# A second group of queries and keys by SyncE, and the first values one score visit earlier

## The chip, the cores and the metric

The kernel runs on one core of a Trainium2 chip. The core has a matrix engine (TensorE, PE in the profile), VectorE (DVE), ScalarE (ACT), GpSimd (POOL) and SyncE (SP), each with its own instruction stream; they wait for each other by semaphores. SP and POOL also issue DMAs. The metric is the device time of one execution in microseconds; the median of several runs is compared.

## The reference

Eight batches of sigmoid attention with 12 heads, 448 positions and head size 64, and behind it a two-layer block with a gate:

```
scores = q k^T / sqrt(64) - log(448)
attn   = 1 / (1 + exp(-scores))            # no sum over a row
x      = attn v, heads side by side        # 3584 x 768
h      = x w_in                            # 3584 x 2048
out    = (h / (1 + exp(-beta h))) w_out    # 3584 x 768
```

All inputs and the output are fp32. There is no softmax: each score is weighed by itself, so values can be taken as soon as a block of scores has passed ACT.

## The kernel before

All matrix products run in fp16 and add up in fp32. A *group* is four heads of one batch (three groups per batch, `QPB` = 3), which fill 128 partitions with 32 rows each when queries and keys are loaded as `[128, 14 x 64]`; a *slot* is two heads, so a group has two slots. `transpose` (line 173) turns 32x32 blocks on DVE and gives `qT` and `kT`; each transposed key tile takes two DVE instructions (lines 186 and 190).

`half_visit(g, c0, second)` (line 237) does half of a group's scores for half of the queries (224 columns): 16 matmuls into two score tiles, and then two ACT activations (`weigh`, line 209) that empty them into fp16. The pool of score tiles has three buffers in the first stage, so the third matmul of a visit waits until an activation two tiles back has ended. `attend(g, c0, n, part)` (line 255) multiplies with the values: 8 matmuls per slot, the last two of them with the last 64 rows of the values, and a DVE copy into `xTs`. `idle_units(n)` (line 518) puts n matmuls on zeros between the visits.

Until line 571 the order is written out by hand, engine by engine in program order (`tc.manual_schedule()`), and this is where the change is. Later stages go by a list of filler units (`dense1`, `dense2`, `strassen`) with costs, laid between the attention visits; none of that is edited.

Loads go two ways. SP's DMAs copy without a change of type: group 0's first half of queries and all of its keys come as fp32 into `staged`, a part of the later `gt` buffer, and are cast by DVE and ACT into `raws[0]` (lines 524 to 527). POOL's DMAs cast on the way (`load_one`, line 106; `load_v`, line 127): groups 1 and 2, then the six DMAs of the first batch's values (lines 131 and 138), then the second halves of the queries, then `w_in` in eight pieces. POOL's DMAs share eight semaphores in turn, so each waits before its issue for the landing of the one eight places ahead.

`double_v_last` (line 140) copies the last 64 rows of the values to the other 64 partitions, which odd slots need. Before, DVE does it after the transpose of group 0's second half of queries, and all values of the first half come after the last score visit of the pass.

Of the kernel before, what the change touches and what calls it, by code (L numbers as in the profile page):

```python
# [9 lines left out]
FP16 = mybir.dt.float16  # L10
# [3 lines left out]
def kernel(  # L14
# [10 lines left out]
    nc = tc.nc  # L25
# [3 lines left out]
    B, H, S, D = q.shape  # L29
    NTOK, DM = out.shape  # L30
    DFF = moe_w_in.shape[1]
    P = 128
    BLK = 32
    HQ = P // BLK
    NB = S // BLK
# [5 lines left out]
    QPB = H // HQ  # L41
# [5 lines left out]
    QH = S // 2  # L47
# [6 lines left out]
    rawp = ctx.enter_context(tc.tile_pool(name="rawp", bufs=3))  # L54
# [29 lines left out]
    def bank(name: str, cols: int = S, hold=None):  # L84
        i = min((i for i in used if i not in held.values()), key=used.get)
        touch(i)
        if hold is not None:
            held[hold] = i
        return psum["one"].tile([P, cols], FP32, tag=f"one{i}", name=name)
# [13 lines left out]
    raws = {}  # L103
    vs = {}

    def load_one(g: int, r: int, c0: int = 0, c1: int = NB):
        b, t = divmod(g, QPB)
        if g not in raws:
            raws[g] = rawp.tile([P, 2, NB, D], FP16, tag="raw", name="raw")
        nc.gpsimd.dma_start(  # L110
            out=raws[g][:, r, c0:c1].rearrange("p c d -> p (c d)"),
            in_=(q, k)[r][b, HQ * t : HQ * (t + 1)].rearrange("h (p c) d -> (h p) (c d)", c=NB)[
                :, c0 * D : c1 * D
            ],
        )
# [8 lines left out]
    def last_base(s: int) -> int:  # L124
        return (s % 2 ^ swapped(s // 2)) * KL

    def load_v(b: int):
        vs[b] = vp.tile([P, H, JF + 1, D], FP16, tag="v16", name="v16")
        rows = v[b].rearrange("h (p c) d -> p h (c d)", c=NB)
        for i in range(HQ):  # L130
            nc.gpsimd.dma_start(  # L131
                out=vs[b][i * BLK : (i + 1) * BLK, :, 0:JF].rearrange("p h j d -> p h (j d)"),
                in_=rows[:, :, JF * i * D : JF * (i + 1) * D],
            )
        rows = v[b].rearrange("h (p c) d -> p h c d", c=NB)
        for c in range(NF, NB):
            lo = (c - NF) * BLK
            nc.gpsimd.dma_start(out=vs[b][lo : lo + BLK, :, JF], in_=rows[:, :, c])

    def double_v_last(b: int):  # L140
        nc.vector.tensor_copy(out=vs[b][KL:P, :, JF], in_=vs[b][0:KL, :, JF])
# [27 lines left out]
    def in_order(b: int, t):  # L169
        t = t.rearrange("p c e -> p (c e)").bitcast(FP32)  # L170
        return t.rearrange("p (q c) -> p c q", c=NB) if b == B - 1 else t

    def transpose(g: int, r: int, c0: int = 0, c1: int = NB):
        raw = raws[g][:, r]
        if r == 0:
            if g not in qT:
                qT[g] = qTp.tile([P, NB * BLK, PAIR], FP16, tag="qT", name="qT")
            nc.vector.transpose(  # L178
                out=in_order(g // QPB, qT[g][:, c0 * BLK : c1 * BLK]),
                in_=raw[:, c0:c1].rearrange("p c d -> p (c d)").bitcast(FP32),  # L180
            )
            return
        kT[g] = kTp.tile([P, S, PAIR], FP16, tag="kT", name="kT")
        to = kT[g].rearrange("p k e -> p (k e)").bitcast(FP32)
        frm = raw.rearrange("p c d -> p (c d)").bitcast(FP32).rearrange("p (c f) -> p c f", c=NB)
        nc.vector.transpose(  # L186
            out=to[:, 0 : JF * P].rearrange("p (j i q) -> p i j q", j=JF, i=HQ),
            in_=frm[:, 0:NF].rearrange("p (i j) f -> p i j f", j=JF),
        )
        nc.vector.transpose(  # L190
            out=to[:, JF * P :], in_=frm[:, NF:].rearrange("p c f -> p (c f)")
        )
# [44 lines left out]
    def half_visit(g: int, c0: int, second: int):  # L237
        slots = (2 * g, 2 * g + 1)
        scos = [score_tile() for _ in slots]
        plan = [(s, jt, sco, jt * QH) for jt in (0, 1) for s, sco in zip(slots, scos)]  # L240
        widths = [S, S]
        if second:
            plan = [(s, 2, sco, 0) for s, sco in zip(slots, scos)]
            plan += [(s, JF, scos[0], QH) for s in slots]
            widths = [S, QH]
        for i in range(0, len(plan), 2):
            for e in range(PAIR):
                for s, jt, sco, u0 in plan[i : i + 2]:
                    for hh in range(2):
                        score(sco, u0, s, jt, hh, e, c0, QH)  # L250
        ats = {id(sco): weigh(sco, n) for sco, n in zip(scos, widths)}
        for s, jt, sco, u0 in plan:
            at_tiles[s, jt, c0] = ats[id(sco)][:, :, u0 : u0 + QH]

    def attend(g: int, c0: int, n: int, part=(0, 1)):
        b, t = divmod(g, QPB)
        if b not in xTs:
            xTs[b] = xTp.tile([P, NHC, S], FP16, tag="xT", name="xT")
        slots = [2 * g + x for x in part]
        avs = [bank("av_ps") for _ in slots]  # L260
        todo = [(s, av, jt) for s, av in zip(slots, avs) for jt in range(JF)]
        for s, av, jt in todo + [(s, av, JF) for s, av in zip(slots, avs)]:
            at = at_tiles.pop((s, jt, c0))
            base, nk = (last_base(s), KL) if jt == JF else (0, P)
            for hh in range(2):
                nc.tensor.matmul(  # L266
                    av[hh * D : (hh + 1) * D, 0:n],
                    vs[b][base : base + nk, 2 * (s % NPAIR) + hh, jt],
                    at[base : base + nk, hh, 0:n],
                    start=(jt == 0),  # L270
                    stop=(jt == JF),
                    tile_position=(base, hh * D),
                )
        for s, av in zip(slots, avs):
            nc.vector.tensor_copy(out=xTs[b][:, s % NPAIR, c0 : c0 + n], in_=av[:, 0:n])  # L275
# [215 lines left out]
    NH = NB // 2  # L491
    firsts = ctx.enter_context(ExitStack())
    share_psum(firsts, 3, 2)
    with tc.manual_schedule():
        raws[0] = rawp.tile([P, 2, NB, D], FP16, tag="raw", name="raw")
        wide = gt.rearrange("p a b -> p (a b)").bitcast(FP32)
        cut = NH * D
        early = [(0, 0, NH), (1, 0, NB)]
        staged = {}
        at = 0  # L500
        for r, c0, c1 in early:
            staged[r] = wide[:, at : at + (c1 - c0) * D]
            at += (c1 - c0) * D
            nc.sync.dma_start(  # L504
                out=staged[r],
                in_=(q, k)[r][0, 0:HQ].rearrange("h (p c) d -> (h p) (c d)", c=NB)[
                    :, c0 * D : c1 * D
                ],
            )
        nc.gpsimd.memset(dummy, 0.0)  # L510
        nc.scalar.activation(out=dummy, in_=dummy, func=AF.Sigmoid, bias=0.0, scale=1.0)
# [6 lines left out]
        def idle_units(n: int):  # L518
            for _ in range(n):
                nc.tensor.matmul(idle, still[:, 0:P], still, start=True, stop=True)  # L520

        idle_units(9)
        raw = raws[0].rearrange("p r c d -> p r (c d)")
        nc.vector.tensor_copy(out=raw[:, 0, 0:cut], in_=staged[0])
        transpose(0, 0, 0, NH)
        nc.scalar.copy(out=raw[:, 1, cut:], in_=staged[1][:, cut:])  # L526
        nc.vector.tensor_copy(out=raw[:, 1, 0:cut], in_=staged[1][:, 0:cut])
        transpose(0, 1)
        for g in range(1, QPB):
            load_one(g, 0, 0, NH)  # L530
            load_one(g, 1)
        load_v(0)
        nc.sync.dma_start(out=beta_in[0:NDC], in_=moe_beta.rearrange("(c p) -> c p", p=P))
        for g in range(QPB):
# [3 lines left out]
        for g in range(1, QPB):  # L538
            transpose(g, 0, 0, NH)
            transpose(g, 1)  # L540

        for g in range(QPB):
            for second in range(2):
                half_visit(g, 0, second)
                if 2 * g + second < 2 * QPB - 1:
                    idle_units(4 if g < QPB - 1 else 2)
        transpose(0, 0, NH, NB)
        double_v_last(0)
        attend(0, 0, QH, (0,))
        attend(0, 0, QH, (1,))  # L550
        half_visit(0, QH, 0)
        attend(1, 0, QH, (0,))
        attend(1, 0, QH, (1,))
# [120 lines left out]
```

## Time and profile before

| | |
|---|---|
| median of 3 runs | 387.36 us (387.35 to 389.22) |
| profiled execution | 387.25 us, span 385.5 us |
| PE busy | 379.1 us (98%) |
| DVE / ACT / POOL busy | 232.6 / 229.6 / 66.4 us |
| DMA, mean over the span | 90 GB/s |
| granted clock of PE | full in every slice |

The profile is of one execution. Its span is 1.75 us shorter than the time of the same execution, which also holds what lies before the first and after the last instruction. Busy times of the engines overlap, so only the chain that ended last, and the waits along it, say what a change can win.

Some events of the first 20 us, from the timelines and the DMA view (us from the start of the span):

| what | issued | landed | used by |
|---|---|---|---|
| group 0, queries / keys (SP) | 0.74 / 1.18 | 3.35 / 4.50 | scores at 5.75 |
| group 1, queries / keys (POOL) | 1.26 / 1.92 | 5.87 / 7.65 | scores at 8.93 |
| group 2, queries / keys (POOL) | 2.44 / 2.96 | 8.26 / 9.4 | scores at 12.14 |
| values, first / last of six (POOL) | 3.49 / 7.96 | 10.3 / 14.05 | values at 14.38 |
| group 0, second half of queries (POOL) | 8.56 | 14.27 | scores at 15.62 |
| `w_in`, first of eight (POOL) | 11.30 | 18.1 | first layer at 19.25 |

### The profile page before, as it was taken

To read this page: it belongs to the slowest core of one execution; us is meant where nothing else is said; L and a number is where in the kernel's file an instruction comes from. 1 tells how busy PE (TensorE), PEld (TensorE's weight loads), DVE (VectorE), ACT (ScalarE), POOL (GpSimd) and SP (SyncE) were. 2 spreads that over 40 slices of the span, in tenths; PEclk is the share of its full clock that TensorE was granted. 3 is DMA by queue.
4 is the path that set the end of the run, shared out by engine and by line. 5 is a ranking of instruction groups with operands and counts; after the bars stand their busy time and mean duration, and the time that the engine had idled before them with its cause. 6 is when DMAs were issued, how large, how long until landed. Compare 5 with 4: busy or idle time off the path is not lost.

```text
span 385.5 us, 7371 instructions
## 1 busy us (share of the span) xinstructions
PE 379.1 (98%) x2987; PEld 190.8 (49%) x2987; DVE 232.6 (60%) x439; ACT 229.6 (60%) x330; POOL 66.4 (17%) x114
## 2 busy tenths in 40 slices
PE   7999999999999999999999999999999999999996
PEld 3477744444554444444554445544455444555553
DVE  4356365875765657555764667755675665655762
ACT  5897855697364785487364783477762777535200
POOL 7832443140110410140110410113100000000000
PEclk9999999999999999999999999999999999999999
DMA  8999999737363930564363660639303300030033
GB/s 165 177 196 204 198 205 202 168 48 73 49 129 76 124 54 2 129 81 40 49 129 83 88 76 8 130 84 118 49 0 83 83 3 2 0 83 0 0 83 122
DMA packets 42401, 34.64 MB, mean 90 GB/s; under 512 B 21872, under 2 KB 38656, under 8 KB 42368
## 3 DMA queue, kind: packets, MB, share of 16 engines
q0 software_dynamic: 36688, 22.47, 42.9%
q1 hardware_dynamic: 5680, 11.71, 11.6%
q8 instruction: 23, 0.38, 0.4%
q14 instruction: 10, 0.08, 0.1%
HBM read 45.62 MB, written 11.01 MB: 147 GB/s over the span
## 4 chain that ended last, share of the span: by engine, by line
PE 95%; ACT 2%; DMA 1%; issue 0%; DVE 0%; SPq 0%; ACTq 0%
PE m_ps L284 38%; PE m_ps L396 29%; PE sco L200 12%; PE av_ps L266 10%; PE m_ps L314 5%; ACT attnT L211 2%; PE idle_ps L520 1%; DMA gt<-in_k_dram 1%; DVE kT L186 0%; ACT raw L526 0%; ACT sg L292 0%; DVE osb L327 0%; DVE gt L295 0%; SPq L504 0%; ACTq L292 0%
## 5 line engine op out<-in xcount | busy, mean ns | idle before, releaser
L211 ACT ACTIVATE attnT<-sco 128x896 f16<-128x896 f32 (+1 forms) x171 | 145.2, 902 | 85.2 <-PE sco L200 84.5
L284 PE MATMUL m_ps<-xT,w_in 128*128 128x448 f16 (+1 forms) x864 | 154.7, 332 | 0.2 <-DVE gt L295 0.2
L295 DVE TENSOR_TENSOR gt<-m_ps,sg 128x448 f16<-128x448 f32 (+1 forms) x144 | 81.8, 573 | 81.1 <-ACT sg L292 77.2
L284 PEld LDWEIGHTS <-w_in 128*128 128x128 f16 x864 | 80.6, 98 | 70.7 <-issue 15.3
L292 ACT ACTIVATE sg<-m_ps,beta_sb 128x448 f32<-128x448 f32 (+1 forms) x144 | 84.5, 597 | 36.2 <-PE m_ps L284 30.9
L396 PEld LDWEIGHTS <-sum 128*128 128x128 f16 x480 | 45.2, 98 | 36.2 <-issue 7.9
L200 PE MATMUL sco<-qT,kT 32*128 32x448 f16 (+3 forms) x864 | 52.1, 340 | 1.4 <-DVE kT L186 1.0
L396 PE MATMUL m_ps<-w_T,sum 128*128 128x384 f16 x288 | 51.6, 327 | 0.0
L110 POOL DMA_DIRECT2D raw<-in_q_dram x26 | 14.3, 550 | 186.2 <-DVE kT L190 179.9
L415 DVE TENSOR_TENSOR osb<-m_ps,osb 128x384 f32<-128x384 f32 x60 | 33.3, 556 | 18.7 <-PE m_ps L396 16.8
L266 PE MATMUL av_ps<-attnT,v 128*64 128x448 f16 (+3 forms) x432 | 42.1, 340 | 0.0
L275 DVE CAST xT<-av_ps 128x448 f16<-128x448 f32 (+1 forms) x54 | 28.8, 568 | 17.8 <-PE av_ps L266 17.7
L385 DVE TENSOR_TENSOR sum<-gt 128x1024 f16<-128x1024 f16 x60 | 39.2, 678 | 0.1
L396 PE MATMUL m_ps<-w_T,gt 128*128 128x384 f16 x192 | 34.2, 326 | 0.0
L396 PE MATMUL m_ps<-w_out,sum 128*128 128x384 f16 x192 | 33.7, 326 | 0.0
L266 PEld LDWEIGHTS <-v 128*64 128x64 f16 (+1 forms) x432 | 19.0, 107 | 24.6 <-issue 17.1
L200 PEld LDWEIGHTS <-kT 32*128 32x128 f16 (+1 forms) x864 | 13.4, 96 | 29.4 <-issue 27.1
L396 PEld LDWEIGHTS <-gt 128*128 128x128 f16 x192 | 18.1, 98 | 14.8 <-issue 3.1
L314 PE MATMUL m_ps<-w_out,gt 128*128 128x384 f16 (+2 forms) x128 | 22.5, 327 | 0.0
L131 POOL DMA_DIRECT2D v<-in_v_dram x32 | 19.8, 631 | 9.8 <-DMA w_in<-in_moe_w_in_dram 5.3
L178 DVE STREAM_TRANSPOSE qT<-raw 128x448 f32<-128x448 f32 (+1 forms) x27 | 16.6, 617 | 4.2 <-DMA raw<-in_q_dram 4.1
L314 PEld LDWEIGHTS <-gt 128*128 128x128 f16 x128 | 11.9, 98 | 10.3 <-issue 3.1
(26 smaller groups left out, 95.3 us busy)
## 6 DMA issues: line engine op xcount, KB each, us to landing
out_dram<-osb SPq DMA_DIRECT2D x98, 96.0 KB, 1.9
raw<-in_k_dram POOLq DMA_DIRECT2D x23, 224.0 KB, 4.5
raw<-in_q_dram POOLq DMA_DIRECT2D x21, 224.0 KB, 3.8
v<-in_v_dram POOLq DMA_DIRECT2D x32, 144.0 KB, 6.2
w_in<-in_moe_w_in_dram POOLq DMA_DIRECT2D x8, 384.0 KB, 10.7
w_out<-in_moe_w_out_dram POOLq DMA_DIRECT2D x4, 768.0 KB, 13.7
v<-in_v_dram POOLq DMA_DIRECT2D x16, 48.0 KB, 6.4
out_dram<-osb SPq DMA_DIRECT2D x2, 384.0 KB, 2.3
```

What stands on the lines that cost most here:

```text
L131: nc.gpsimd.dma_start(out=vs[b][i * BLK : (i + 1) * BLK, :, 0:JF].rearrange("p h j d -> p h (j d)"), in_=rows[:, :, JF * i * D : JF * (i + ...
L200: nc.tensor.matmul(sco[base : base + nk, hh, u0 : u0 + n], kT[g][lo : lo + BLK, jt * P : jt * P + nk, e], qT[g][lo : lo + BLK, c0 : c0 + n ...
L211: nc.scalar.activation(out=at[:, :, 0:n], in_=sco[:, :, 0:n], func=AF.Sigmoid, bias=NEG_LOG_S, scale=MSCALE,)
L266: nc.tensor.matmul(av[hh * D : (hh + 1) * D, 0:n], vs[b][base : base + nk, 2 * (s % NPAIR) + hh, jt], at[base : base + nk, hh, 0:n], start ...
L275: nc.vector.tensor_copy(out=xTs[b][:, s % NPAIR, c0 : c0 + n], in_=av[:, 0:n])
L284: nc.tensor.matmul(m1[:, 0:n], w_in16[:, hc, dc * P : (dc + 1) * P], xTs[b][:, hc, c0 : c0 + n], start=(hc == 0), stop=(hc == NHC - 1),)
L292: nc.scalar.activation(out=sg[:, 0:n], in_=m1[:, 0:n], func=AF.Sigmoid, bias=0.0, scale=beta_sb[:, dc : dc + 1])
L295: nc.vector.tensor_tensor(out=gt[:, dc, off : off + n], in0=m1[:, 0:n], in1=sg[:, 0:n], op=ALU.mult)
L314: nc.tensor.matmul(m2, gt[:, dc, cols(t)], w_out16[:, dc, lo:hi], start=(dc == 0), stop=(dc == NDC - 1),)
L385: nc.vector.tensor_tensor(out=sums[t, i], in0=x, in1=y, op=op)
L396: nc.tensor.matmul(m2, (x if op is None else sums[t, i])[:, dc], w[:, dc], start=first and dc == 0, stop=(dc == ND - 1), skip_group_check= ...
L415: nc.vector.tensor_tensor(out=out, in0=in0, in1=in1, op=op)
```

## The change

Group 1's first half of queries and its keys are no longer cast on the way by POOL's DMAs. SP loads them as fp32 behind group 0's, into the next part of the `gt` buffer, and DVE casts them into `raws[1]` (448 and 896 elements per partition) ahead of its transposes of that group. POOL's queue begins with group 2. In the last group of the first pass, the two idle matmuls between its visits are left out; the values of group 0's first slot take that place, ahead of the last score visit, and those of its second slot follow that visit. DVE doubles the last value rows ahead of the transpose of group 0's second half of queries.

```diff
-        raws[0] = rawp.tile([P, 2, NB, D], FP16, tag="raw", name="raw")
+        for g in range(2):
+            raws[g] = rawp.tile([P, 2, NB, D], FP16, tag="raw", name="raw")
...
-        early = [(0, 0, NH), (1, 0, NB)]
+        early = [(g, r, (NH, NB)[r] * D) for g in range(2) for r in range(2)]
...
-        for r, c0, c1 in early:
-            staged[r] = wide[:, at : at + (c1 - c0) * D]
-            at += (c1 - c0) * D
+        for g, r, n in early:
+            staged[g, r] = wide[:, at : at + n]
+            at += n
             nc.sync.dma_start(
-                out=staged[r],
-                in_=(q, k)[r][0, 0:HQ].rearrange("h (p c) d -> (h p) (c d)", c=NB)[
-                    :, c0 * D : c1 * D
-                ],
+                out=staged[g, r],
+                in_=(q, k)[r][0, g * HQ : (g + 1) * HQ].rearrange(
+                    "h (p c) d -> (h p) (c d)", c=NB
+                )[:, 0:n],
             )
...
         transpose(0, 1)
-        for g in range(1, QPB):
-            load_one(g, 0, 0, NH)
-            load_one(g, 1)
+        raw = raws[1].rearrange("p r c d -> p r (c d)")
+        nc.vector.tensor_copy(out=raw[:, 0, 0:cut], in_=staged[1, 0])
+        nc.vector.tensor_copy(out=raw[:, 1], in_=staged[1, 1])
+        load_one(2, 0, 0, NH)
+        load_one(2, 1)
         load_v(0)
...
+        double_v_last(0)
+        transpose(0, 0, NH, NB)
         for g in range(QPB):
             for second in range(2):
                 half_visit(g, 0, second)
-                if 2 * g + second < 2 * QPB - 1:
-                    idle_units(4 if g < QPB - 1 else 2)
-        transpose(0, 0, NH, NB)
-        double_v_last(0)
-        attend(0, 0, QH, (0,))
-        attend(0, 0, QH, (1,))
+                if g < QPB - 1:
+                    idle_units(4)
+                else:
+                    attend(0, 0, QH, (second,))
         half_visit(0, QH, 0)
```

More of the change, by code (lines that the diff above doesn't have):

```diff
@@ L523 @@
         raw = raws[0].rearrange("p r c d -> p r (c d)")
-        nc.vector.tensor_copy(out=raw[:, 0, 0:cut], in_=staged[0])
+        nc.vector.tensor_copy(out=raw[:, 0, 0:cut], in_=staged[0, 0])
         transpose(0, 0, 0, NH)
-        nc.scalar.copy(out=raw[:, 1, cut:], in_=staged[1][:, cut:])
-        nc.vector.tensor_copy(out=raw[:, 1, 0:cut], in_=staged[1][:, 0:cut])
+        nc.scalar.copy(out=raw[:, 1, cut:], in_=staged[0, 1][:, cut:])
+        nc.vector.tensor_copy(out=raw[:, 1, 0:cut], in_=staged[0, 1][:, 0:cut])
         transpose(0, 1)
-        for g in range(1, QPB):
-            load_one(g, 0, 0, NH)
-            load_one(g, 1)
+        raw = raws[1].rearrange("p r c d -> p r (c d)")
[3 more added lines that the diff above has]
+        load_one(2, 1)
         load_v(0)
```

## The prediction

> **What bounds the kernel now.** I read the page first (busy time and the chain that ended last), then busy time by stage, then the chain of the first 50 us in order of time, and last the timelines of ACT, DVE and POOL around the lines that move.
>
> ```profile
> span 385.5 us, 7371 instructions
> ...
> PE 379.1 (98%) x2987; PEld 190.8 (49%) x2987; DVE 232.6 (60%) x439; ACT 229.6 (60%) x330; POOL 66.4 (17%) x114
> ...
> PE 95%; ACT 2%; DMA 1%; issue 0%; DVE 0%; SPq 0%; ACTq 0%
> ```
>
> TensorE (PE) is busy nearly throughout and holds 95% of the chain. By stage (PE is the second number and the first busy time):
>
> ```profile
> 0.00:16.00 16.00, 13.65 (x155) 5.64 (x155) 5.92 (x17) 11.26 (x15) 12.36 (x24) 1.00 1.14 173
> 16.00:45.00 29.00, 28.96 (x366) 21.07 (x356) 16.07 (x47) 22.77 (x42) 11.08 (x18) 1.00 1.41 194
> ...
> 90.00:370.00 280.00, 280.00 (x2041) 135.72 (x2039) 175.14 (x313) 164.88 (x231) 28.66 (x50) 1.00 0.37 62
> ```
>
> From 16 us on PE stops for almost nothing, so what the change does before 16 us is carried to the end one for one, and nothing later can be won. The chain there (start, length, what):
>
> ```profile
> 1.18 3.31 DMA gt<-in_k_dram
> ...
> 8.03 0.97 PE idle_ps L520 x4
> 8.99 0.63 PE sco L200 x16
> ...
> 12.79 0.93 ACT attnT L211
> 13.71 0.04 issue
> 13.75 0.69 PE sco L200 x14
> 14.45 1.24 PE av_ps L266 x16
> 15.69 0.51 PE sco L200 x14
> 16.20 1.86 PE av_ps L266 x24
> ```
>
> The reader is to see that scores wait for ScalarE (ACT) to empty a score tile (12.79 to 13.71), and only then come the first values (14.45). ACT itself runs without a real pause here: its 12 activations of the first pass fill 9.49 us from 6.36. The last lines are of the timelines of ACT, DVE and POOL (start, length, in brackets the wait before):
>
> ```profile
> 14.50 1.35 ACT L211 ACTIVATE attnT<-sco 128x896 f16<-128x896 f32 x2
> 7.69 0.58 DVE L186 STREAM_TRANSPOSE kT<-raw 128x384 f32<-128x384 f32 x1 [1.42 <-DMA raw<-in_k_dram]
> 14.28 0.41 DVE L178 STREAM_TRANSPOSE qT<-raw 128x224 f32<-128x224 f32 x1 [4.14 <-DMA raw<-in_q_dram]
> 3.49 2.50 POOL L131 DMA_DIRECT2D v<-in_v_dram  x4
> 7.96 0.61 POOL L138 DMA_DIRECT2D v<-in_v_dram  x1 [1.21 <-DMA raw<-in_k_dram]
> ```
>
> **PE: two idle matmuls less, eight value matmuls earlier.** Before, from the end of the score visit at 12.76: two idle matmuls 0.54, two score matmuls and the wait for ACT until 13.75 (0.45), the rest of the visit 0.63 (14.38), 16 value matmuls 1.24 (15.62), the next score visit 0.51 (16.13). After: 8 value matmuls 0.62 (13.38); the same wait until 13.75, since the ninth activation, begun at 12.79, still frees its tile then; 0.63 to 14.38; 8 value matmuls 0.62 (15.00). Now the next visit comes too early. Its third matmul needs the tile of the eleventh activation, which begins at 14.50; the ninth took 0.96 from its start to the release of PE, so 15.46; the 14 matmuls left at 0.51/16 each take 0.45: 15.91. The gain is 16.13 - 15.91 = 0.22 us, out of the 0.54 + 0.18 (the wait proper) = 0.72 that stood there. The rest turns into a new wait for ACT at about 15.1.
>
> **SP and DVE: does group 1 come in time?** SP issues two more DMAs (0.38 and 0.42 us in the rows of group 0) at about 1.6 and 2.1; beta's moves from 1.65 to about 2.5, landed in 3.8, and is first used at 19.67, so it costs nothing. The queue moved 672 KB of group 0 from 1.75 to about 3.9, at 360 to 460 GB/s once it ran; at 400 the next 672 KB take 1.7, ending at 5.6, and landing follows by 0.6 as for group 0's keys (4.50 against 3.9): 6.2. That is the lower bound. The upper: if POOL's queue takes half from 3.9 on, 672 KB at 200 GB/s take 3.4, landing 7.9. After landing DVE casts 128x896: not in the trace; 128x448 took 0.395, of which 0.18 is fixed (transposes of 224 and 448 elements took 0.41 and 0.63), so 0.61, at most 2 x 0.395 = 0.79. Then transposes: 0.41, and 0.63 from kT's start to PE (5.12 to 5.75 for group 0). In all 1.71 (1.89). PE wants group 1 at 8.93, so landing by 7.22 (7.04) costs nothing and 7.9 costs 0.7 to 0.85. I take the low value: POOL's first data appear at 3.7, 2.4 us after its first issue at 1.26, where on idle queues they came 1.2 after (154.56, data at 155.8). So POOL's queue moved nothing while SP's streamed. The query cast (0.395) sits before this and is covered by the wait for the keys. Queued behind the casts on DVE are only group 2's transposes, wanted at 12.14 and ready at 10.13 before: 2 us of cover.
>
> **POOL: are the values there at 12.8?** POOL loses two issues (0.67 + 0.54), so the six value DMAs start at 2.44, not 3.49, and all go out by about 6.0, as the ring of eight no longer makes the last wait for group 1's keys (1.21 in the row above). The DMA view has the last value load issued at 7.96 and landed 6.1 later, 14.05. Ahead of it stood 1344 KB on this queue, now 1008; 336 KB at the 180 GB/s of 8 to 12 us are 1.9 less, and the start comes 1.7 later behind SP's stream: 13.85. But POOL's queue ran slowly from 3.65 to 7.0 (0.44 MB, 131 GB/s) while POOL was writing; with the writing done before it starts, 0.44 MB at 180 saves 0.9: 12.95. I take the middle, 13.4, since the row of 154.56 shows both, about 120 GB/s at first and 190 to 215 within a microsecond. The need: the last two matmuls of the early values (at 13.23) wait for v's last rows; after them 0.15, a score visit of 0.69 and 0.05 of latency must be over at 14.5, so landing by 13.6 costs nothing. Each microsecond later costs one, and the gain is gone at 13.82. Queries of the second half are issued once group 2's queries land, about as before, landed at 14.27 and are wanted at 15.0: cover 0.3 after 0.35 of copy and 0.41 of transpose. Weights of the first layer landed at 18.1 and are used at 19.25; their queue position in time is unchanged.
>
> **Sum.** -0.22. The profiled execution (387.25, span 385.5) would be 387.03; the median of the runs, 387.36, stands 0.11 above it, so 387.1. A measurement of this kernel tells some 0.5% (1.9 us) from no change, far more than this.
>
> [...] When casts ran at 3.35 and 4.52, the value issues beside them took 0.616 to 0.670, and 0.61 without. [...] SP's stream left POOL's queue waiting 1.2 us. [...]
>
> **The rivals.**
> 1. The values are late and PE, in order, holds the last score visit behind them. For: before, they landed only at 14.05. Against: 336 KB less ahead. At 13.95 it gives +0.1, at 14.6 +0.8 (388.2); slower than before from 13.82 on.
> 2. Group 1 is late. Under a fair share it lands at 7.9: 0.7 to 0.85 late, less 0.22: +0.5 to +0.6 (387.9). For: eight DMAs are queued beside it. Against: the 3.7.
> [...]
> 4. ACT's release is not the bound and the whole 0.72 is won: 386.6. Against: the 13.71 line.
> That the change does not do what it says is excluded by the order of the instructions: loads, casts and value matmuls stand where the text puts them.
>
> **Chances.** Forecast (within 0.25 of 387.1) 0.47; rival 1 0.25, of it 0.05 beyond 389.3; rival 2 0.13, 0.01 beyond; rival 3 0.08, 0.04 beyond; rival 4 0.02; 0.05 for a gain over 0.5% that no row shows. So faster 0.05, same 0.85, slower 0.10. The range runs from rival 4's 386.6 to 388.6, which takes in rival 2 and most of rival 1; the forecast's own is 386.9 to 387.4.
>
> **What would show it.** Right: score visits of group 1 still at 8.9, a wait for ACT of about 0.3 at 15.1, values of the second group at 15.9. [...]

## The result, and the profile after

The changed kernel takes 390.72 us (median of 6, 389.45 to 392.01) against 387.36 us before, a ratio of 1.0077 with a 95% interval of 1.0056 to 1.0098: slower, by 2.2 to 3.8 us, where 0.22 us less was forecast, too little to tell from no change. The profiled execution is the lowest of the six, 389.45 us with a span of 387.7 us, so the profile shows 2.2 us of the loss, and the other executions lose more. First the page of the kernel after, with the same lines as shown of before:

```profile
span 387.7 us, 7370 instructions
...
PE 381.1 (98%) x2985; PEld 190.9 (49%) x2985; DVE 233.1 (60%) x441; ACT 229.4 (59%) x330; POOL 65.4 (17%) x112
...
PE 93%; ACT 2%; DMA 2%; DVE 1%; issue 0%; SPq 0%; ACTq 0%
```

The span grew by 2.2 us, and the chain now holds 2% of DMA and 1% of DVE where it held 1% and none. Busy time by stage (start and end of the stretch, its length, busy time and instructions of PE, PE's weight loads, DVE, ACT and POOL, then the granted clock, the DMA share and GB/s) says where:

```profile
0.00:16.00 16.00, 13.58 (x115) 4.89 (x116) 5.92 (x17) 8.90 (x12) 11.18 (x22) 1.00 1.11 191
16.00:45.00 29.00, 28.67 (x376) 20.87 (x374) 15.84 (x45) 24.31 (x45) 10.62 (x17) 1.00 1.39 193
90.00:370.00 280.00, 280.00 (x2049) 135.08 (x2046) 174.56 (x313) 165.62 (x232) 28.77 (x50) 1.00 0.38 63
```

From 90 to 370 us PE is as full as before. In the first 16 us it issued 115 matmuls where it had issued 155, in nearly the same busy time, since some of them were slow (below). The chain of the first 50 us of the kernel after:

```profile
2.12 7.87 DMA gt<-in_k_dram
9.99 0.02 issue
10.01 0.63 DVE raw L532
10.64 0.32 DVE qT L178
10.96 0.47 DVE kT L186
11.43 0.05 issue
11.47 0.58 PE sco L200 x15
...
15.30 2.64 ACT attnT L211 x3
17.94 0.04 issue
17.98 0.57 PE sco L200 x11
18.55 1.87 PE av_ps L266 x24
```

The line to look at is the first. Group 1's keys, issued by SP at 2.12, land at 9.99; through POOL they had landed at 7.65. Behind them stand the cast and the transposes, and group 1's scores begin at 11.47, 2.54 later than the 8.93 of before. The values of the second group, which began at 16.13, begin at 18.48: 2.35 later. From there on the two kernels run in step, and the spans differ by 2.2.

In this execution not all of the 2.54 is the keys'. PE's first matmuls were slow: the four idle matmuls at 6.86 took 1.89 us, where they take 1.04 in the kernel before. Before (start, length, in brackets the wait):

```profile
6.26 1.04 PE L520 MATMUL idle_ps<-still 128*128 128x512 f16 x4
...
8.93 0.69 PE L200 MATMUL sco<-qT,kT 32*128 32x224 f16 x16
```

After:

```profile
6.86 1.89 PE L521 MATMUL idle_ps<-still 128*128 128x512 f16 x4
...
9.69 1.34 PE L521 MATMUL idle_ps<-still 128*128 128x512 f16 x4
11.47 0.58 PE L200 MATMUL sco<-qT,kT 32*128 32x224 f16 x16 [0.44 <-DVE kT L186]
```

PE was through with its own work only at 11.03 and waited 0.44 us for the keys. A second profile of the changed kernel, of an execution of 390.69 us and so close to the median, shows the keys' part by itself. There PE ran at its usual pace, was through at 9.72, and waited 2.97 us for keys that DVE could begin to cast only at 11.23 (DVE, then PE):

```profile
11.23 0.63 DVE L532 CAST raw<-gt 128x896 f16<-128x896 f32 x1 [2.59 <-DMA gt<-in_k_dram]
...
8.69 1.04 PE L521 MATMUL idle_ps<-still 128*128 128x512 f16 x4
12.69 0.58 PE L200 MATMUL sco<-qT,kT 32*128 32x224 f16 x16 [2.97 <-DVE kT L186]
```

### The profile page after: what moved, and what is told of

Same layout as the page of the kernel before. It is cut to its first block, busy times and chain, and to the rows that moved or that the text cites. A ratio compares the mean times of both kernels' runs of the same rounds, so it can differ in the third digit from the quotient of the medians.

```text
span 387.7 us, 7370 instructions
## 1 busy us (share of the span) xinstructions
PE 381.1 (98%) x2985; PEld 190.9 (49%) x2985; DVE 233.1 (60%) x441; ACT 229.4 (59%) x330; POOL 65.4 (17%) x112
## 4 chain that ended last, share of the span: by engine, by line
PE 93%; ACT 2%; DMA 2%; DVE 1%; issue 0%; SPq 0%; ACTq 0%
PE m_ps L284 38%; PE m_ps L396 29%; PE sco L200 11%; PE av_ps L266 10%; PE m_ps L314 5%; ACT attnT L211 2%; DMA gt<-in_k_dram 2%; PE idle_ps L521 1%; SPq L505 0%; DVE raw L532 0%; DVE kT L186 0%; ACT sg L292 0%; DVE osb L327 0%; DVE gt L295 0%; DVE qT L178 0%
## 5 line engine op out<-in xcount | busy, mean ns | idle before, releaser
L200 PE MATMUL sco<-qT,kT 32*128 32x448 f16 (+3 forms) x864 | 53.0, 344 | 1.8 <-DVE kT L186 1.2
L178 DVE STREAM_TRANSPOSE qT<-raw 128x448 f32<-128x448 f32 (+1 forms) x27 | 16.5, 615 | 0.1
```

Source lines behind the costliest of these rows:

```text
L200: nc.tensor.matmul(sco[base : base + nk, hh, u0 : u0 + n], kT[g][lo : lo + BLK, jt * P : jt * P + nk, e], qT[g][lo : lo + BLK, c0 : c0 + n ...
```

## The experiments

The theory formed from the two traces (A): SP's and POOL's loads share the DMA engines, so group 1's keys come late, and their lateness is the loss. The rivals: the new order costs PE the time (B); SP's queue is slow for its second pair of loads by itself (C). A further theory, on the spread between executions, is called D below.

**Each half of the change alone.** First the order without the loads:

```diff
+        double_v_last(0)
+        transpose(0, 0, NH, NB)
         for g in range(QPB):
             for second in range(2):
                 half_visit(g, 0, second)
-                if 2 * g + second < 2 * QPB - 1:
-                    idle_units(4 if g < QPB - 1 else 2)
-        transpose(0, 0, NH, NB)
-        double_v_last(0)
-        attend(0, 0, QH, (0,))
-        attend(0, 0, QH, (1,))
+                if g < QPB - 1:
+                    idle_units(4)
+                else:
+                    attend(0, 0, QH, (second,))
```

> The loads of the kernel before, with only the order of the change: no idle matmuls in the last group, the first slot's values ahead of the last score visit, the last value rows doubled before the transpose. Theory A (the whole loss is group 1's keys landing late, because SP's and POOL's queues share the DMA engines): scores of group 1 start at 8.9 us as before; the last value rows land at about 14.05, so the early values hold the last visit for 0.2 to 0.5 us; 387.3 to 387.9 us in all. Theory B (the new order costs PE the time, by values that block the visit behind them): 389 us or more.

Measured: 387.68 us (10 executions) against 387.70, ratio 1.0001 (0.9985 to 1.0017). The order alone costs and wins nothing that can be measured. B falls.

Then the loads and casts of the change with the order of before (the same lines the other way round):

> The loads and casts of the change with the order of the kernel before. Theory A: group 1's keys land at about 10.0 us, its scores start at about 11.5, and the time is that of the changed kernel plus the 0.2 us of the order, 389.6 to 392 us. Theory B: 387.2 to 387.6 us.

Measured: 392.74 us (4 executions, 389.83 to 393.88) against 387.70, ratio 1.011 (1.0065 to 1.0155). The whole loss comes with the loads, and more than expected. DVE could begin the cast of the keys only at 10.99 in its profile, and group 1's scores began at 12.45. This profile also shows something that the profile of the changed kernel hides, a fall of the granted clock. By stretch, the clock being the number ahead of the last two:

```profile
8.00:9.00 1.00, 1.00 (x12) 0.31 (x4) 0.37 (x1) 1.00 (x2) 0.00 (x0) 1.00 1.23 246
9.00:10.00 1.00, 0.21 (x1) 0.00 (x0) 0.03 (x1) 0.65 (x2) 0.00 (x0) 1.00 1.54 193
10.00:11.00 1.00, 0.00 (x0) 0.00 (x0) 0.01 (x1) 0.00 (x0) 0.55 (x1) 1.00 1.61 188
11.00:12.00 1.00, 0.00 (x0) 0.00 (x0) 1.00 (x3) 0.00 (x0) 0.24 (x1) 0.53 1.82 175
12.00:13.00 1.00, 0.55 (x16) 0.44 (x16) 1.00 (x4) 0.00 (x0) 1.00 (x2) 0.50 1.63 187
...
16.00:17.00 1.00, 1.00 (x11) 0.31 (x4) 0.00 (x0) 0.73 (x1) 1.00 (x2) 0.50 1.31 157
17.00:18.00 1.00, 1.00 (x7) 0.17 (x9) 0.00 (x0) 0.62 (x2) 1.00 (x3) 0.56 1.32 165
18.00:19.00 1.00, 1.00 (x19) 0.39 (x19) 0.00 (x0) 0.43 (x1) 0.85 (x2) 1.00 1.29 146
```

PE stood idle from 9.2 to 12.45, waiting for the keys. About two microseconds into the pause the clock fell to half and stayed there until about 17.9, for 6.8 us: the price of the pause goes on after it ends.

**The queues apart.** POOL's queue is held back until group 1's keys are in:

```diff
+        nc.gpsimd.tensor_copy(out=dummy, in_=staged[1, 1][:, 0:1])
         load_one(2, 0, 0, NH)
```

> The changed kernel, but POOL reads one element of group 1's staged keys before its first DMA, so its queue is empty while SP's four loads run. Theory A: alone on the engines, group 1's keys land at 6.2 to 6.6 us and its scores start at 8.9 to 9.0; the values start some 5 us later and their last rows land at 15.5 to 16.5, which now costs 2 to 3 us, so the time stays at 389 to 390.5. Rival C (SP's queue is slow for its second pair of loads by itself, whatever POOL does): keys still land at 9 or later.

Measured, in one execution: DVE begins the cast of the keys at 6.78 instead of 10.01, and group 1's scores begin at 8.96. C falls, and A's first half holds: the same four loads on the same queue, alone, bring the keys 3.2 us earlier. The timelines of DVE and PE (start, length, in brackets the wait before):

```profile
6.78 0.63 DVE L532 CAST raw<-gt 128x896 f16<-128x896 f32 x1 [0.65 <-DMA gt<-in_k_dram]
...
8.96 0.69 PE L200 MATMUL sco<-qT,kT 32*128 32x224 f16 x16
...
16.83 0.48 PE L266 MATMUL av_ps<-attnT,v 128*64 128x224 f16 x6 [3.77 <-DMA v<-in_v_dram]
```

The time is 394.84, some 4 us more than expected: PE waited 3.77 for the values, whose last rows came at 17.7 instead of 15.5 to 16.5, and the granted clock averaged 0.987 over the execution: at 18.03 a score visit of 16 matmuls took 1.07 us, at 12.48 it had taken 0.58.

**Less on SP.** Group 1's keys go back to POOL's queue, in its first place, and only the queries (224 KB) stay on SP:

```diff
-        early = [(g, r, (NH, NB)[r] * D) for g in range(2) for r in range(2)]
+        early = [(0, 0, NH * D), (0, 1, NB * D), (1, 0, NH * D)]
...
-        nc.vector.tensor_copy(out=raw[:, 1], in_=staged[1, 1])
+        load_one(1, 1)
         load_one(2, 0, 0, NH)
```

> The changed kernel with group 1's keys back on POOL's queue, in its first place, and only group 1's queries (224 KB) on SP. Theory A: sharing the engines with 224 instead of 672 KB, the queries land at 6 to 7 us, the keys at 6.5 to 7.6, group 1's scores start at 8.9 to 9.1, the last value rows land at 13.4 to 14; 387.0 to 387.5 us. Theory B: 389 us or more. Rival C: queries at 8 or later, scores at 9.5 or later, 388 us.

Measured: 388.28 us (10 executions, 387.38 to 389.37) against 387.70, ratio 1.0008 (0.9992 to 1.0024). The time is above what A gave, and the times of landing were missed by more: DVE could cast the queries only at 9.34, where 6 to 7 was expected. A load of a third of the size, alone on its queue from 3.9 on, still took until 9.3. The scores began at 10.80 in the profile, where PE, slow at first in this execution too, came to them without a wait. These numbers are the ones that C had given (8 or later, 9.5 or later, 388). But C has the queue slow whatever POOL does, and in the run before SP's second pair came early as soon as POOL's queue was empty. What is wrong in A is the size: the share that SP gets beside POOL is smaller than equal parts of 400 GB/s. From 5 to 8 us SP's packets took 27.9% of the engines' time here, POOL's 71.8%.

**POOL a little later.** POOL's queue waits for group 0's queries only:

```diff
+        nc.gpsimd.tensor_copy(out=dummy, in_=staged[0, 0][:, 0:1])
         load_one(2, 0, 0, NH)
```

> The changed kernel, but POOL reads one element of group 0's staged queries (landed at 3.35 to 3.5) before its first DMA, so its queue starts at about 4.0 and its first data come at 5.2 or later, when SP's loads are nearly over. Theory A (the queues take turns on the engines): group 1's keys land at 6.3 to 7.0 us and its scores start at 8.9 to 9.1; the last value rows land at 13.5 to 15, so 387.1 to 388.5 us in all, 2 to 3 us below the changed kernel. If it isn't the turns: keys at 9 or later and 389 us or more.

Measured: 388.19 us (12 executions) against 387.50 for before and 390.69 for the changed kernel on the same chip; ratio to before 1.0033 (1.0004 to 1.0061). The cast of the keys begins at 6.88 in the profile, as A expects. Group 1's scores begin at 9.30, 0.2 later than A gave, but PE came to them only then and did not wait for the keys. What is left is the values, which now land at 14.38 and hold the last score visit, as the first rival of the prediction had it:

```profile
13.14 0.48 PE L266 MATMUL av_ps<-attnT,v 128*64 128x224 f16 x6
14.43 0.28 PE L266 MATMUL av_ps<-attnT,v 64*64 64x224 f16 x2 [0.81 <-DMA v<-in_v_dram]
14.64 0.70 PE L200 MATMUL sco<-qT,kT 32*128 32x224 f16 x16
```

Three of the twelve stand at 390.77 to 392.33 with a granted clock of 0.987 to 0.991; the other nine have a median of 388.0.

The same loads with the order of before, where the values come after the last score visit:

> POOL's queue started after group 0's queries, as in the run before, but with the order of the kernel before (values after the last score visit, two idle matmuls). Theory A: keys at 6.8 to 6.9 us; the last value rows land at 14.0 to 14.6, and the values start at 14.4 to 15 without holding a score visit: 387.2 to 387.8 us for most executions, 0.3 to 0.6 below the same loads with the new order, and fewer executions with a granted clock below 0.995. If the late values are not the rest of the loss: 388.2 us as with the new order.

Measured: 387.69 us (11 executions, 387.13 to 387.98) against 387.60, ratio 0.9998 (0.9986 to 1.0009), and no granted clock below 0.998. With the queues apart and no early values, the loss is gone altogether. This also says that group 1's loads on SP and its casts on DVE cost nothing by themselves that can be measured.

**Lateness without the loads.** The kernel before, with eight unneeded transposes on DVE ahead of group 1's:

```diff
+        junk = const.tile([P, 448], FP32, name="junk")
+        for _ in range(8):
+            nc.vector.transpose(out=junk, in_=raws[0][:, 1].rearrange("p c d -> p (c d)").bitcast(FP32))
         for g in range(1, QPB):
             transpose(g, 0, 0, NH)
```

> The kernel before with eight unneeded transposes of 128x448 on DVE (some 4.6 us) ahead of group 1's, so that group 1's scores start at 11.0 to 11.7 us as in the changed kernel, with the loads of the kernel before. Theory A with D: 389.4 to 392 us, with the same spread and clocks as the changed kernel, since only the lateness counts. If the loss lies elsewhere in the change: below 388.5 us.

Measured: 392.13 us (6 executions, 390.32 to 392.76), ratio 1.0100 (1.0072 to 1.0127). The transposes took 5.36 us together, more than meant, and the scores began at 12.04 in the profile. The loads were those of before, so the lateness alone makes a loss of this size, whoever causes it. The median lies a little above the 392 that A with D gave. Five of the six had a granted clock of 0.990 to 0.996, and the one at 1.000 was the lowest.

The changed kernel again, on the same chip as the last one and the first run below:

> The changed kernel again, on the same chip as the others: 389.4 to 392 us.

Measured: 390.69 us (7 executions, 389.57 to 391.64). The four with a granted clock of 1.000 lie between 389.57 and 390.69, the three at 0.995 to 0.996 between 390.89 and 391.64. At a full clock the landing of the keys makes a spread as well: in the two profiles of this kernel group 1's scores began at 11.47 and 12.69, 1.22 us apart, and the times of these executions, 389.45 and 390.69, are 1.24 apart.

**Keeping PE busy while it waits.** The slow end of the spread goes with the granted clock. Theory D: PE's pause lets the clock fall in some executions.

```diff
-                    idle_units(4)
+                    idle_units(12 if (g, second) == (0, 1) else 4)
```

> The changed kernel with 12 idle matmuls instead of 4 ahead of group 1's first scores, so that PE is busy for most of the time in which it waits for group 1's keys. Theory D (over the 2.3 us of the late keys, the idle PE lets its clock fall in some executions, and that is the spread of 389.4 to 392.0): the times draw together at 389.2 to 390.0 us with a granted clock of 1.000. Without D: the same spread, up to 392.

Measured: 390.55 us (8 executions): seven between 389.60 and 390.91 with a clock of 0.999 or 1.000, one at 392.63 with 0.995. D gave 389.2 to 390.0 and a full clock for all. But PE still paused for 1.02 us in the profile, so D was not settled. With 16 idle matmuls:

> The changed kernel with 16 idle matmuls ahead of group 1's first scores instead of 4, so that PE waits for the keys for less than 0.5 us. Theory D: granted clock 0.998 or more in every execution and no time above 391.0; 389.5 to 390.6 us. Without D: some executions at 391.5 to 392.6 with a granted clock below 0.997.

Measured: 389.89 us (5 executions, 389.83 to 390.67), all with a clock of 0.998 or more. D holds as far as five executions can say. What remains, 1.0057 times the kernel before (1.0035 to 1.008), is the late keys without the clock, and some of it the idle matmuls themselves: in the profile the cast began at 9.96, so the scores could have begun at about 11.4 (in the changed kernel 1.46 us after the cast), but the sixteen matmuls ran until 12.04. The profiles of all runs point the same way: after pauses of 3.24 and 3.77 us (the loads alone, the queues apart) the clock fell, after pauses of 0.44 to 2.97 us it did not.

**Is it the length of a packet?** Group 1's keys in four DMAs, each with a quarter of every row:

```diff
+            cuts = 4 if (g, r) == (1, 1) else 1
+            for i in range(cuts):
+                w = n // cuts
-            nc.sync.dma_start(
-                out=staged[g, r],
+                nc.sync.dma_start(
+                    out=staged[g, r][:, i * w : (i + 1) * w],
...
```

> The changed kernel with group 1's keys loaded by four SP DMAs of 896-byte rows instead of one of 3584-byte rows: the same bytes in four times as many packets. Theory A in its narrow form (the two queues take turns packet by packet, so the bytes of a packet set the share): each turn moves a quarter, the keys land clearly later, at 11.5 us or more. If the queues share by bytes or by time: 9.8 to 10.8 us, as before.

Measured, in one execution: the cast of the keys begins at 10.78, 390.05 us. Whole rows gave 10.01, 11.23, 10.99, 10.58 and 9.96 in five profiles with POOL's loads beside them, so short rows changed nothing that one execution can show. (SP also spent 2.30 us on the four issues, against 0.43 on the one.) The narrow form of A, turns by packet with the bytes of a packet setting the share, is not supported.

**One more try at the kernel before.** Eleven idle matmuls at the start instead of nine:

> The kernel before with 11 idle matmuls at the start instead of 9, so that PE does not pause between them and the first scores. Theory D: the executions of the kernel before at 389.0 to 389.6 us, five of twenty in the last comparison, are those in which the clock rises only after the first visits; with PE busy without a gap they are fewer, and the others stay at 387.2 to 387.9. Without D: still a quarter at 389.0 and above.

Measured: 387.78 us (11 executions, 387.23 to 388.44) against 387.60 (21 executions, of which two at 389.11 and 389.79); ratio 0.9999 (0.9985 to 1.0013). None at 389 and above, but two in 21 is too few to tell that from chance: inconclusive. No kernel here beat the kernel before.

## Why the prediction was wrong

**The step that failed: when group 1's keys come in.** The prediction took 6.2, the lower of its two bounds, and gave 7.9 as the upper. Measured: 9.99, above both. The choice of the lower one rested on one reading, that POOL's first data came at 3.7, 2.4 us after the first issue, and on its conclusion, "POOL's queue moved nothing while SP's streamed". In the kernel after, SP's stream goes on past that time, and POOL's data come all the same. The DMA view of the kernel before from 4.5 to 8 us (packets, MB, share of 16 engines):

```profile
q0 software_dynamic: 427, 0.53, 105.5%
q1 hardware_dynamic: 16, 0.00, 0.9%
```

And of the kernel after, from 3.9 to 4.0 us and then from 4.5 to 8 us:

```profile
q1 hardware_dynamic: 16, 0.04, 91.6%
q0 software_dynamic: 5, 0.00, 29.6%
```

```profile
q0 software_dynamic: 212, 0.26, 50.3%
q1 hardware_dynamic: 242, 0.57, 49.3%
```

POOL's queue (q0) starts at 3.9 with SP's (q1) in full stream, and then each holds half of the engines' time. SP moved 0.57 MB in 3.5 us, 163 GB/s. POOL's 0.26 MB are counted after the cast to half the bytes (group 1's queries stand in the DMA view with 112 KB on POOL's queue before, with 224 KB on SP's after), so it read 0.52 MB, about as much. One coincidence, the end of one stream and the start of the other, had been read as a cause.

The upper bound failed in its size. It was half of 400 GB/s, the rate of SP's first pair. Both queues together read 0.57 + 0.52 MB in 3.5 us, 311 GB/s, and with POOL held back SP's second pair alone moved 0.68 MB from 3.9 to 6.1, 309 GB/s. Half of 310 is 155 GB/s, and 672 KB (0.69 MB) at 155 take 4.4 us: 8.3 for the data instead of 7.3. The rest is a tail: from 8 to 10 us SP moved its last 0.11 MB, as POOL's packets, now short and many, went by (288 in the ninth microsecond, 466 in the tenth). Why the tail is so slow is not shown. Short packets on POOL's side alone do not explain it: with the keys in quarter rows SP moved 0.26 MB in the same two microseconds.

The unit in which the two queues share the engines is not shown. The packets were 242 on SP's queue to 212 on POOL's in those 3.5 us of the kernel after, and 160 to 255 from 5 to 8 us in the run with the queries alone. With rows of a quarter the length the keys came no later: their cast began at 10.78, with whole rows at 9.96 to 11.23.

**The second rival was the right mechanism, and its price too low.** It had the keys 0.7 to 0.85 us late, and an idle PE ahead of group 1's scores, with DVE waiting for SP's queue, is what the profiles show. PE waited 2.97 us in the execution close to the median. Without the fall of the clock this part of the loss is at most 2.3 us in the runs with sixteen idle matmuls, 389.89 against 387.60, since these matmuls held the scores at the end themselves. From landing to scores it took 1.48 us; the prediction's 1.71 is 0.06 more than the parts it names (0.61, 0.41 and 0.63), which decided nothing.

**What the prediction left out: the granted clock.** It priced a late group at its lateness and no more. The granted clock also fell in some executions. In the loads alone it fell to half 1.9 us into a pause of 3.24 us and stayed there for 6.8 us. In the queues apart, after a pause of 3.77 us, PE was slow from 18.03 on (1.07 us for 16 score matmuls that had taken 0.58), and the mean clock of 0.987 over the span of 393.1 us would be some 10 us at half (an estimate: twice 0.013 of the span). After a pause of 2.97 us, in the second profile of the changed kernel, the clock did not fall. How long a pause it takes is not shown. Which executions fall varies. In the repeated kernel a low clock went with about 1 us more: 391.06 is the middle of its three executions with a low clock, 390.1 that of the other four.

**What held.** The count of PE: from the end of the third group's first visit (15.27) to the second group's values (18.48) it took 3.21 us, forecast 3.15, before 3.37. The new wait for ACT is there (17.51 and two matmuls, then 17.98, with 0.20 us of waiting). ACT was also the limit that kept the early values from winning more than 0.2 us. The order alone fits this but cannot prove it: its time is that of the kernel before within the noise, and in its profile it took 7.04 us from group 1's scores (9.25) to the second group's values (16.29), before 7.20 (8.93 to 16.13). The cast of the keys took 0.63, forecast 0.61. Rival 3, which has 0.08 of the chances, stands for casts that hold POOL's issues; no run shows a hold of microseconds. POOL's four value issues took 2.49 us beside two of group 0's casts, and 2.50 before, also beside two. In the run that holds POOL until group 0's queries (POOL a little later) both of group 1's own casts, at 5.76 and 6.88, fell among these issues, and they took 2.54. The values landed at 14.0, forecast 13.4; with the keys so late it did not matter, and where the keys were in time (POOL a little later) the wait of 0.81 came, and the first rival's price held: 0.56 us for a landing at 14.38 (one for one from 13.82), measured 0.5 (388.0 against 387.50 for the executions at a full clock).

## What to carry to other kernels

A load moved to a second queue was not moved out of the way of the first: beside POOL's loads the cast of group 1's keys began at 10.01, with POOL's queue held back at 6.78. Where both queues had work, half of the read rate that the engines reached in that stage (here 310 GB/s, not the 400 of SP's first pair) gave the earliest landing, not the likely one: by it, with 0.6 us from the last data to the landing, 672 KB would have landed at 8.9 and 224 KB at about 6, and they came at 10.0 and 9.3. Check that a landing well behind that still meets its first use. Where a bound rests on one coincidence in time, keep the other bound as the forecast until a second row says the same. And where PE would wait for about 3 us, count the clock too: it fell in the profiles with pauses of 3.24 and 3.77 us and not in the one with 2.97, and in the loads alone it stayed at half for 5.4 us after the pause.

## What the runs showed of the hardware that had not been expected

- POOL's first load shows its first data 2.4 to 2.6 us after its issue at 1.26, with SP's queue busy for longer or not. Issued at 4.01 the first data come 1.6 to 1.8 us after, at 7.41 on idle queues 1.4 us. What delays the first one at the start of a kernel stays open.
- 224 KB on SP beside POOL's loads took nearly as long (9.3) as 672 KB (10.0). SP's share of the engines fell from 40.8% between 5 and 6 us to 27.3, 15.5 and 3.5% in the three microseconds behind it, though POOL's packets under 512 B became many (152) only after 8 us. What drags the end of such a load stays open.
- POOL's copy of one element, in the runs that hold its queue back, took 0.32 us at 3.50 (POOL a little later) and 0.56 us at 6.89 (the queues apart), where it ran beside VectorE's cast of the keys and ended at 7.45, 0.04 us after it. What sets its time is not shown.
- The start of the clock varies between executions. In the first profile of the changed kernel the first 13 idle matmuls were slow (nine took 4.02 us at 1.19, against 3.58 in the kernel before; four took 1.89 us at 6.86, against 1.04 later, and 1.89 at a granted clock of 0.50 in the loads alone). The trace holds its first record of a full clock at 10.35 us, in the kernel before at 4.19; the views show 1.00 where there is no record, so a clock "full in every slice" says nothing of the time ahead of it. The slow matmuls filled the wait, PE paused only 0.44 us before group 1's scores, and the clock did not fall. Where it had risen early, as in the profile of the loads alone, the pause was 3.24 us and it fell, and the time was 392.91 instead of 389.45. What decides when the clock rises is not shown.
